# A decode backward kernel: dw2 and the last head's dV stored by GpSimd scatters that skip the first partitions, and plain transfers for these

## Chip, cores and metric

The kernel runs on 1 core of a Trainium2 chip. The metric is the device time of one execution in microseconds: 404.78 us before the change, as the median of 3 runs (404.63 to 404.84).

## The reference

The program is the gradient of a small mixed layer for one token. Attention over a cached K and V of 32 heads x 4096 positions x 128 (bf16) is mixed by a sigmoid gate with a dense layer (640 to 1728 to 640, mish). It returns the output and nine gradients.

```python
def _A_ref(x, k_cache, v_cache, wq, wo):
    q = ...(x @ wq) split into 32 heads
    scores = jnp.einsum("bhqd,bhkd->bhqk", q, k_cache) * (Dh ** -0.5)
    p = _softmax(scores, axis=-1)
    o = jnp.einsum("bhqk,bhkd->bhqd", p, v_cache)
    return o.reshape(B, Sq, H * Dh) @ wo

def _B_ref(x, w1, b1, w2):
    h = x @ w1 + b1
    act = h * jnp.tanh(softplus(h))
    return act @ w2

out = g * a + (1 - g) * b          # g = sigmoid(sum(x * gate_w))
_out, _vjp = jax.vjp(_f, A_x, A_k_cache, A_v_cache, A_wq, A_wo, B_w1, B_b1, B_w2, gate_w)
return (out, *_vjp(grad_out))
```

Most of the bytes are K and V (32 MB each, read) and dK and dV (32 MB each, written). dV of a head is the outer product of its 4096 probabilities and its 128 values of do; dw2 (1728 x 640) is the outer product of the activations and the scaled gradient.

## The kernel before

**Tiling.** A head's K or V is a tile of 128 partitions x 32 positions x 128 (1 MB; partition p holds positions 32p to 32p + 31, so a partition's row is 8,192 B, contiguous in memory). Heads run one after the other in a software pipeline written out by hand: the loop body of head h (lines 743 to 853) transposes K and V of head h + 1 and part of h + 2 on TensorE (`k_pe`, `v_pe`, line 515), evicts them on ScalarE (`ev`, line 524), does the softmax of head h on VectorE, and multiplies out dV (`dv_out`) and dK (`dk_out`) in halves on VectorE (`outer`, line 598).

**Stores.** `out_half` (line 602) picks the output tile, and after the second half stores it through SyncE's queue (line 616). Tiles come from `outs` (4 buffers, o_sb); for the last heads the freed input buffers Kn and Vn are used (dK of heads 28 to 30, dV of heads 29 to 31), so that these need not wait for an earlier store. dK of head 31 goes through o_sb again.

**Queues.** SyncE issues nearly all transfers in program order: loads of K and V four heads ahead, weights, and all large stores. GpSimd issues a few small ones: b1, the rows of h (lines 410, 412), the last 64 rows of dw2 (line 800), db1 (line 802), and at the end three stores of 5 rows each, taken from fin_rows (lines 920 to 922). Each engine takes its instructions in order.

**dw2.** w2 lies in w2_sb as 13 blocks of 640 in each of 128 partitions (a row of 16,640 B, contiguous in memory), and a 14th block of 64 partitions. `m_dw2(fc)` (line 503, on ScalarE) overwrites block fc by the gradient; `dw2_some(2)` at the end of each loop body does two of them, once w2 is no longer read, counting up from `dw2_next[0]`. At head 28 (`h == H - 4`, line 796) all blocks must be done; SyncE then stores blocks 0 to 3, 4 to 7 and 8 to 12 (line 799), GpSimd the 14th and db1. GpSimd's queue is free by then, so line 800 goes out as soon as its data is ready.

**The end.** After the loop: softmax, dV and dK of head 31, then the last dwq (line 377) and dwo (line 386), and the vectors out, dx and dgate, which are gathered in fin_rows.

The order of instructions on each engine is the program's (`manual_schedule`); waits between engines, and between transfers that touch the same memory, are put in by the framework.

Of the kernel before, what the change touches and what calls it, by code (L numbers as in the profile page):

```python
# [8 lines left out]
ALU = mybir.AluOpType  # L9
# [7 lines left out]
def kernel(  # L17
# [24 lines left out]
    nc = tc.nc  # L42
    P = 128
    _, H, Sk, Dh = A_k_cache.shape
# [8 lines left out]
    FR = F // P  # L53
    FM = FR * P
# [4 lines left out]
    W2P = [(0, 4), (4, 8), (8, FR)]  # L59
# [17 lines left out]
    dw2_v = out_8[0:FM, :].rearrange("(p fc) n -> p fc n", p=P)  # L77
# [11 lines left out]
    const = ctx.enter_context(tc.tile_pool(name="const", bufs=1))  # L89
# [59 lines left out]
    w2_sb = const.tile([P, FCN, D], BF16, name="w2_sb")  # L149
    for a, b in W2P:  # L150
# [10 lines left out]
        out=ident_bf[:], in_=ident_bf[:], compare_op=ALU.not_equal, fill=1.0,  # L161
        base=0, pattern=[[-1, P]], channel_multiplier=1,
# [20 lines left out]
    nc.vector.memset(aT_acc[:], 0.0)  # L183
    bT = const.tile([P, RC], F32, name="bT")
    dx_parts = const.tile([P, RC, NG + 3], F32, name="dx_parts")

    p4b, ds4b = [], []
    qz = const.tile([P, G, 2, 2, 16], BF16, name="qz")
# [57 lines left out]
    def g_qpair_cp(g):  # L246
        pair_cp(qz, groups[g].pop("pair"), 4)

    def g_docol(g):
        groups[g]["col"] = col_mm(groups[g]["do_row"])  # L250

    def g_dopair(g):
        groups[g]["pair"] = pair_mm(groups[g].pop("col"))
# [160 lines left out]
    def m_np(fc):  # L414
        return P if fc < FR else FT
# [60 lines left out]
    def m_diag():  # L476
        nc.vector.tensor_copy(dh_bf[:, 0:FR], dh32[:, 0:FR])
        nc.vector.tensor_copy(dh_bf[0:FT, FR:FCN], dh32[0:FT, FR:FCN])
        nc.gpsimd.tensor_tensor(diag3, ident_bf[:].unsqueeze(2).to_broadcast([P, P, FR]),
                                dh_bf[:, 0:FR].unsqueeze(1).to_broadcast([P, P, FR]), ALU.mult)  # L480
        nc.gpsimd.tensor_tensor(mjunk[0:FT, FM:F], ident_bf[0:FT, 0:FT],
                                dh_bf[0:FT, FR:FCN].to_broadcast([FT, FT]), ALU.mult)
# [18 lines left out]
    def m_dw2(fc):  # L501
        n = m_np(fc)
        nc.scalar.activation(w2_sb[0:n, fc, :], db_bc[0:n, :], ACT.Copy, scale=act_f[0:n, fc:fc + 1])
# [14 lines left out]
    def ev():  # L518
        trq.pop(0)()
# [6 lines left out]
    def k_pe(h, c):  # L526
        if h < H:
            tr_pe(h, kts, KT, c)

    def v_pe(h, c):  # L530
        if h < H:
            tr_pe(h, vts, VT, c)
# [32 lines left out]
    def softmax(h):  # L565
        mx = s_ps.tile([P, P + 2], F32, name="mx", tag="mx")
        nc.tensor.transpose(mx[:, 0:P], dgms.pop(h)[:].to_broadcast([P, P]), ident_f[:])  # L567
        negM = small.tile([P, 1], F32, name="negM", tag="negM")
        nc.vector.tensor_reduce(negM[:], mx[:, 0:P], axis=AX.X, op=ALU.max, negate=True)  # L569
        return mx, negM  # L570

    def exps(h, negM):
        es[h] = small.tile([P, J], BF16, name="e_bf", tag="e_bf")
        zds[h] = small.tile([P, 2], F32, name="zd", tag="zd")
        nc.scalar.activation(es[h][:], sd[h][0], ACT.Exp, bias=negM[:], scale=scale, accum_out=zds[h][:, 0:1])  # L575
# [21 lines left out]
    def outer(dst, col4, row, a, b):  # L597
        nc.vector.tensor_tensor(  # L598
            dst[:, a:b, :].rearrange("p j (k t) -> p j k t", t=4),
            row.rearrange("p (k t) -> p k t", t=4).unsqueeze(1).to_broadcast([P, b - a, Dh // 4, 4]),  # L600
            col4[:, a:b, :].unsqueeze(2).to_broadcast([P, b - a, Dh // 4, 4]), ALU.mult)

    o_t = {}

    def out_half(w, h, dst, col4, row, k):
        hh = h % G
        if k == 0:
            if w == "k" and H - KBUFS <= h < H - 1:
                o_t[w, h] = kv_in.tile([P, J, Dh], BF16, name="Kn", tag="Kn")
            elif w == "v" and h > H - VBUFS:  # L610
                o_t[w, h] = kv_in.tile([P, J, Dh], BF16, name="Vn", tag="Vn", bufs=VBUFS)
            else:
                o_t[w, h] = outs.tile([P, J, Dh], BF16, name="o_sb", tag="o_sb")
        outer(o_t[w, h], col4, row[:, hh * Dh:(hh + 1) * Dh], k * JH, (k + 1) * JH)
        if k == 1:
            nc.sync.dma_start(dst[h], o_t.pop((w, h))[:])

    def dv_out(h, k):
        out_half("v", h, dVv, p4s[h], groups[h // G]["do_row"], k)
# [1 line left out]
    def dk_out(h, k):  # L621
        if h >= 0:
            out_half("k", h, dKv, ds4s[h], groups[h // G]["qs_row"], k)
# [12 lines left out]
    def dqo_red(h, x):  # L636
        if h >= 0:
            v = x[:].rearrange("p t r -> p (t r)")[:, 3:3 + 4 * (P - 1)].rearrange("p (s q) -> p s q", q=P - 1)
            nc.vector.tensor_reduce(groups[h // G]["dqo"][:, :, h % G],  # L639
                                    v[:, :, 0:P - 1:32].rearrange("p s (i c) -> p i s c", i=2),  # L640
                                    axis=AX.XY, op=ALU.add)
# [6 lines left out]
    m_cost = dict(h=0.8, b1=0.8, act=0.9, b=0.5, dh=0.9, diag=0.5, bc=0.5, dx=0.9, dw1=0.5, gap=0.0)  # L648
    m_fn = dict(h=m_h, b1=lambda i: (m_b1(), m_abs()), act=m_act, b=m_b, dh=m_dh,
                diag=lambda i: m_diag(), bc=m_bc, dx=m_dx, dw1=m_dw1)  # L650
    dw2_next = [0]

    def mlp_some(budget, pause=True):
        spent = 0.0
# [88 lines left out]
    for h in range(H - 1):  # L743
        g, hh = h // G, h % G
        nx, pv = g + 1 < NG, g > 0
        k_pe(h + 1, 2)
        ev()
        mx, negM = softmax(h)
        if hh == 3 and nx:
            g_qpair_cp(g + 1)  # L750
            g_docol(g + 1)
        dqo_red(h - 1, xs[h])
        k_pe(h + 1, 3)
        ev()
        exps(h, negM)
        dk_out(h - 1, 1)
        v_pe(h + 1, 0)
        if hh == 2 and nx:
            g_q(g + 1)
        v_pe(h + 1, 1)  # L760
        if hh == 3 and nx:
            g_dopair(g + 1)
            g_dopair_cp(g + 1)
        k_rows(h + 1)
        ev()
        ev()
        pjs(h)
        v_pe(h + 1, 2)
        ev()
        zd_mm(h, mx)  # L770
        if hh == 0 and pv:
            f_new(g - 1)
            f_diag(g - 1)
        elif h >= 2:
            mlp_some(0.9, False)
        v_pe(h + 1, 3)
        ev()
        probs(h, mx)
        if hh == 0 and pv:
            f_o4(g - 1)  # L780
            f_o4c(g - 1)
            f_bc(g - 1)
        dv_out(h, 0)
        k_pe(h + 2, 0)
        dq_o(h)
        v_rows(h + 1)
        rw_cp(h + 1)
        if h + 2 < H:
            ev()
        dv_out(h, 1)  # L790
        load_k(h + KBUFS)
        load_v(h + VBUFS)
        k_pe(h + 2, 1)
        if h + 2 < H:
            ev()
        if h == H - 4:
            assert dw2_next[0] == FCN
            for a, b in W2P:
                nc.sync.dma_start(dw2_v[:, a:b, :], w2_sb[:, a:b, :])
            nc.gpsimd.dma_start(out_8[FM:F, :], w2_sb[0:FT, FR, :])  # L800
            assert not any(k == "bc" for k, _ in mq)
            nc.gpsimd.dma_start(db1_row, dh_bc[0:1, :])
        if h == H - 2:
            assert not mq
            nc.sync.dma_start(dw1_v[:, 0:3, :], w1_sb[:, 0:3, :])
            nc.sync.dma_start(dw1_v[:, 3:RC, :], w1_sb[:, 3:RC, :])
        dk_out(h, 0)
        x_tr(h + 1)
        maxes(h + 1)
        if hh == 0:  # L810
            if nx:
                g_new(g + 1)
            if pv:
                l_pe(g - 1, 0, G)
                l_add(g - 1, g - 1, True)
                for t in range(G):
                    f_dwo(g - 1, t)
                f_dwo_st(g - 1)
                for c in range(2):
                    f_dx(g - 1, c)  # L820
                    f_dwq(g - 1, c)
        if hh == 1:
            if pv:
                for c in range(2, RC):
                    f_dx(g - 1, c)
                    f_dwq(g - 1, c)
                f_dwq_st(g - 1)
            if nx:
                w_pe("o", g + 1, 0)
                ev()  # L830
                w_pe("o", g + 1, 1)
                ev()
        if hh == 2:
            if g + 2 < NG:
                load_wo(g + 2)
            if not nx:
                for k in range(NWT):
                    w_pe("q", g, k)
                    ev()
            else:  # L840
                w_pe("o", g + 1, 2)
                ev()
                g_do(g + 1)
                g_qcol(g + 1)
                g_qpair(g + 1)
        if hh == 3:
            if g % 2 == 0 and g + 4 <= NG:
                load_wqp(g // 2 + 1)
            if nx:
                g_qs(g + 1)  # L850
        if h >= 2:
            mlp_some(0.9 if hh < 2 else 1.8)
            dw2_some(2)

    g, h = NG - 1, H - 1
# [97 lines left out]
```

## Time and profile before

| | us |
|---|---|
| median of the runs | 404.78 |
| profiled execution | 404.96 |
| its span | 403.18 |
| PE busy in the span | 305.9 |
| DVE busy | 287.9 |
| ACT busy | 232.4 |
| POOL busy | 11.8 |
| DMA, mean | 408 GB/s over 164.55 MB |
| last issue of dV (head 31) on SyncE | 384.71 |
| last issue of dwo on SyncE | 390.73 |
| first issue of fin_rows on GpSimd | 393.67 |

The span runs from the first instruction of the program to the last one; the profiled execution's own time is 1.78 us longer. An issue is the moment at which an engine's sequencer starts a transfer; its landing is told by a semaphore that each of the 16 DMA engines raises when its share is in, so that a transfer has 16 landing records, and it has landed with the last. The DMA engines work on shares of every transfer: with 128 rows each has 8. Queue q1 is SyncE's, q0 is GpSimd's.

### The profile page before, as it was taken

To read this page: it belongs to the slowest core of one execution; us is meant where nothing else is said; L and a number is where in the kernel's file an instruction comes from. 1 tells how busy PE (TensorE), PEld (TensorE's weight loads), DVE (VectorE), ACT (ScalarE), POOL (GpSimd) and SP (SyncE) were. 2 spreads that over 40 slices of the span, in tenths; PEclk is the share of its full clock that TensorE was granted. 3 is DMA by queue.
4 is the path that set the end of the run, shared out by engine and by line. 5 is a ranking of instruction groups with operands and counts; after the bars stand their busy time and mean duration, and the time that the engine had idled before them with its cause. 6 is when DMAs were issued, how large, how long until landed. Compare 5 with 4: busy or idle time off the path is not lost.

```text
span 403.2 us, 7688 instructions
## 1 busy us (share of the span) xinstructions
PE 305.9 (76%) x2930; PEld 207.0 (51%) x2945; DVE 287.9 (71%) x808; ACT 232.4 (58%) x468; POOL 11.8 (3%) x29
## 2 busy tenths in 40 slices
PE   2979989787897985876887779876886977677640
PEld 1556646464565663544555447544555645464420
DVE  2217738868678875769897956896997985679780
ACT  2466757754676563753668667765767655375220
POOL 3000001000000000000001200000000000000001
PEclk9999999988999998989998997988999899889555
DMA  7999999999999999999999999999999999999894
GB/s 274 428 416 423 417 424 415 417 423 424 422 422 426 423 414 424 424 418 428 422 423 428 424 418 424 427 418 423 422 419 424 425 417 425 426 422 377 360 389 153
DMA packets 28708, 164.55 MB, mean 408 GB/s; under 512 B 2991, under 2 KB 3056, under 8 KB 12288
## 3 DMA queue, kind: packets, MB, share of 16 engines
q1 hardware_dynamic: 28256, 163.97, 98.1%
q8 instruction: 23, 0.38, 0.4%
q0 software_dynamic: 384, 0.10, 0.1%
q14 instruction: 13, 0.11, 0.1%
q10 hardware_dynamic: 32, 0.01, 0.0%
HBM read 82.03 MB, written 82.03 MB: 407 GB/s over the span
## 4 chain that ended last, share of the span: by engine, by line
DMA 42%; PE 25%; DVE 22%; ACT 6%; issue 2%; POOL 0%; POOLq 0%; SPq 0%; DVEq 0%; ACTq 0%
DMA out_dram<-o_sb 40%; PE tr L515 9%; DVE o_sb L598 9%; PE rw L538 3%; PE rw L631 3%; DVE junk L362 3%; DMA wq_p<-in_A_wq_dram 2%; PE x L555 2%; DVE wq_p L372 2%; ACT rw_sb L549 2%; ACT do_row L266 2%; PE tr L324 2%; PE do_ps L263 1%; PE h_ps L405 1%; DVE mjunk L494 1%
## 5 line engine op out<-in xcount | busy, mean ns | idle before, releaser
L524 ACT COPY T<-tr 128x512 f32<-128x512 f32 x256 | 138.0, 595 | 53.0 <-PE tr L515 38.3
L598 DVE TENSOR_TENSOR o_sb<-qs_row,ds 128x2048 bf16<-128x2048 bf16 x58 | 70.8, 1220 | 37.6 <-DMA out_dram<-o_sb 37.5
L515 PE MATMUL tr<-ident_f,Kn 128*128 128x128 f32 x512 | 85.6, 295 | 5.8 <-DVE rw L508 5.8
L515 PE MATMUL tr<-ident_f,Vn 128*128 128x128 f32 x512 | 84.5, 299 | 6.6 <-ACT T L524 6.0
L515 PEld LDWEIGHTS tr<-ident_f,Vn 128*128 128x128 f32 x512 | 63.4, 154 | 27.3 <-PE tr L515 12.1
L515 PEld LDWEIGHTS tr<-ident_f,Kn 128*128 128x128 f32 x512 | 61.1, 149 | 23.2 <-PE rw L631 14.1
L598 DVE TENSOR_TENSOR o_sb<-do_row,p 128x2048 bf16<-128x2048 bf16 x58 | 68.2, 1218 | 0.0
L549 ACT COPY rw_sb<-rw 128x512 f32<-128x512 f32 x33 | 19.4, 587 | 51.2 <-PE rw L538 49.0
L631 PE MATMUL rw<-Kn,ds 128*4 128x512 bf16 x256 | 35.9, 405 | 6.4 <-DVE ds L593 5.7
L631 PE MATMUL rw<-Vn,p 128*4 128x512 bf16 x256 | 35.9, 405 | 0.0
L567 PE MATMUL mx<-ident_f,m_s 128*128 128x128 f32 x32 | 10.1, 316 | 29.7 <-DVE m_s L563 29.6
L555 PE MATMUL x<-ident_f,rw_sb 128*128 128x128 f32 x132 | 22.5, 295 | 4.4 <-ACT rw_sb L549 1.4
L362 DVE SCALAR_TENSOR_TENSOR junk<-wq_p,dq_bc 128x512 bf16<-128x512 bf16 x35 | 23.9, 684 | 0.0
L538 PE MATMUL rw<-T,qz 128*32 128x512 bf16 x256 | 22.3, 426 | 0.0
L575 ACT ACTIVATE e_bf<-x,negM 128x32 bf16<-128x32 f32 x32 | 9.3, 292 | 22.4 <-DVE dqo L639 22.1
L567 PEld LDWEIGHTS mx<-ident_f,m_s 128*128 128x128 f32 x32 | 4.5, 142 | 34.0 <-DVE m_s L563 33.9
L538 PE MATMUL rw<-T,doz 128*32 128x512 bf16 x256 | 21.4, 411 | 0.8 <-ACT T L524 0.8
L380 ACT ACTIVATE wo_g<-da_bc,o 128x640 bf16<-128x640 bf16 x28 | 20.9, 816 | 1.2 <-PE ax_ps L350 1.2
L583 PE MATMUL mx<-zd,ones_f 128*128 128x2 f32 x64 | 11.2, 245 | 13.5 <-DVE pj L579 13.4
L555 PEld LDWEIGHTS x<-ident_f,rw_sb 128*128 128x128 f32 x132 | 14.5, 145 | 13.2 <-ACT rw_sb L549 13.2
L569 DVE TENSOR_REDUCE negM<-mx 128x1 f32<-128x128 f32 x32 | 9.2, 288 | 16.1 <-PE mx L567 16.1
L631 PEld LDWEIGHTS <-ds 128*4 128x4 bf16 x256 | 9.1, 85 | 22.2 <-DVE ds L593 11.4
(174 smaller groups left out, 367.6 us busy)
## 6 DMA issues: line engine op xcount, KB each, us to landing
out_dram<-o_sb SPq DMA_DIRECT2D x58, 1024.0 KB, 16.6
Kn<-in_A_k_cache_dram SPq DMA_DIRECT2D x32, 1024.0 KB, 16.8
Vn<-in_A_v_cache_dram SPq DMA_DIRECT2D x32, 1024.0 KB, 17.3
wq_p<-in_A_wq_dram SPq DMA_DIRECT2D x4, 1280.0 KB, 8.7
wo_g<-in_A_wo_dram SPq DMA_DIRECT2D x8, 640.0 KB, 17.6
out_dram<-wo_g SPq DMA_DIRECT2D x8, 640.0 KB, 18.3
out_dram<-wq_p SPq DMA_DIRECT2D x4, 1280.0 KB, 16.3
out_dram<-Kn SPq DMA_DIRECT2D x3, 1024.0 KB, 11.4
```

Source lines behind the costliest of these rows:

```text
L362: nc.vector.scalar_tensor_tensor(jq[:], in0=wqs[g][:, c, :], scalar=1.0, in1=groups[g]["dq_bc"][:], op0=ALU.mult, op1=ALU.mult, accum_out= ...
L380: nc.scalar.activation(wos[g][:, hh, :], da_bc[:], ACT.Copy, scale=groups[g]["o4"][:, hh:hh + 1])
L515: nc.tensor.transpose(tp[:, t, :], words[:, t * P:(t + 1) * P], ident_f[:])
L524: nc.scalar.copy(T[h][:, (3 - c) * (TB // 2):(4 - c) * (TB // 2), :], tp[:])
L538: nc.tensor.matmul(rw[32 * c:32 * (c + 1), :], lhsT=z[:, par, :, :].rearrange("p m u -> p (m u)"), rhs=Tb[:, c, par, :, :], start=first an ...
L549: nc.scalar.copy(rw_sb[h][:].rearrange("p t r -> p (t r)"), rw[:])
L555: nc.tensor.transpose(xs[h][:, 3 - j, :], t[:, j, :], ident_f[:])
L567: nc.tensor.transpose(mx[:, 0:P], dgms.pop(h)[:].to_broadcast([P, P]), ident_f[:])
L575: nc.scalar.activation(es[h][:], sd[h][0], ACT.Exp, bias=negM[:], scale=scale, accum_out=zds[h][:, 0:1])
L583: nc.tensor.matmul(mx[:, P:P + 2], lhsT=ones_f[:], rhs=zds[h][:], start=True, stop=True)
L598: nc.vector.tensor_tensor(dst[:, a:b, :].rearrange("p j (k t) -> p j k t", t=4), row.rearrange("p (k t) -> p k t", t=4).unsqueeze(1).to_br ...
L631: nc.tensor.matmul(rw[32 * c:32 * c + 4, :], lhsT=c4[:, 4 * jb:4 * jb + 16].rearrange("p (j t) -> p t j", t=4)[:, 0, :], rhs=N[:, jb:jb + ...
```

## The change

The three stores of dw2 by SyncE become one scatter by GpSimd with one row of 16,640 B for each partition, and the store of dV of head 31 becomes another, with one row of 8,192 B for each partition. A scatter takes the target row of each partition from a list in SBUF, `rowids`: p for dw2, 31 x 128 + p for dV. In the first 8 entries (dw2) or 16 entries (dV) the list holds a row beyond the bound (8192), and such a row is not written. A plain transfer, issued by GpSimd right behind the scatter, writes these rows. The list is made on GpSimd at the start by two instructions.

`m_dw2` of block 0 is held back: `dw2_next` starts at 1, and block 0 is scaled at head 28, right before the stores. In GpSimd's order come then: the 64 rows of the 14th block, the scatter and the plain rows of dw2, db1, the scatter and the plain rows of dV, and the three stores of fin_rows.

The target of the dV scatter is all of dV seen as 4096 rows, that of its plain rows the first 16 of head 31; the framework lets the scatter wait for the earlier stores into dV, and the plain rows for the scatter.

```diff
+    SKIP = (8, 16)
+    rowids = const.tile([P, 2], mybir.dt.int32, name="rowids")
+    nc.gpsimd.iota(rowids[:], pattern=[[(H - 1) * P, 2]], base=0, channel_multiplier=1)
+    nc.gpsimd.affine_select(out=rowids[:], in_=rowids[:], compare_op=ALU.is_ge, fill=float(2 * H * P),
+                            base=-SKIP[0], pattern=[[SKIP[0] - SKIP[1], 2]], channel_multiplier=1)
+
+    def scat_st(i, rows, lim, dst, src):
+        ids = rowids[:, i:i + 1].bitcast(mybir.dt.uint32)
+        nc.gpsimd.indirect_dma_start(out=rows, out_offset=bass.IndirectOffsetOnAxis(ap=ids, axis=0), in_=src,
+                                     in_offset=None, bounds_check=lim - 1, oob_is_err=False)
+        nc.gpsimd.dma_start(dst[0:SKIP[i]], src[0:SKIP[i]])
...
         if k == 1:
-            nc.sync.dma_start(dst[h], o_t.pop((w, h))[:])
+            t = o_t.pop((w, h))
+            if (w, h) == ("v", H - 1):
+                scat_st(1, out_3.rearrange("b h (p j) d -> (b h p) (j d)", p=P), H * P,
+                        dst[h].rearrange("p j d -> p (j d)"), t[:].rearrange("p j d -> p (j d)"))
+            else:
+                nc.sync.dma_start(dst[h], t[:])
...
-    dw2_next = [0]
+    dw2_next = [1]
...
         if h == H - 4:
             assert dw2_next[0] == FCN
-            for a, b in W2P:
-                nc.sync.dma_start(dw2_v[:, a:b, :], w2_sb[:, a:b, :])
+            m_dw2(0)
             nc.gpsimd.dma_start(out_8[FM:F, :], w2_sb[0:FT, FR, :])
+            rows = out_8[0:FM, :].rearrange("(p fc) n -> p (fc n)", p=P)
+            scat_st(0, rows, P, rows, w2_sb[:, 0:FR, :].rearrange("p fc n -> p (fc n)"))
             assert not any(k == "bc" for k, _ in mq)
             nc.gpsimd.dma_start(db1_row, dh_bc[0:1, :])
```

## The prediction

> **What bounds the kernel now.** I read the slices of the page first, then its chain of waits, then the last 30 us in windows, and last SyncE's final waits.
>
> ```profile
> span 403.2 us, 7688 instructions
> ...
> DMA  7999999999999999999999999999999999999894
> ...
> DMA 42%; PE 25%; DVE 22%; ACT 6%; issue 2%; POOL 0%; POOLq 0%; SPq 0%; DVEq 0%; ACTq 0%
> ```
>
> The 16 DMA engines are full from the second slice to the last but two. Up to 344 us the chain goes through stores (o_sb buffers that come free late), after that through computation alone. What ends the span is seen in the windows (columns: stretch, length, five engines' busy time, granted clock, DMA share, GB/s):
>
> ```profile
> 369.00:371.00 2.00, 0.27 (x3) 0.08 (x1) 1.87 (x6) 1.33 (x5) 0.00 (x0) 1.00 0.60 252
> ...
> 376.00:388.00 12.00, 7.59 (x68) 5.01 (x67) 8.95 (x26) 3.30 (x9) 0.00 (x0) 0.50 1.01 409
> ...
> 397.00:402.00 5.00, 0.00 (x0) 0.00 (x0) 0.00 (x0) 0.00 (x0) 0.00 (x0) 0.50 0.07 26
> ```
>
> From 397 to 402 us the share is 0.07, one engine of 16 (0.0625), at 26 GB/s. SyncE's last waits say the same: after the small fin_rows stores it still waits 1.0 us and 1.5 us for two large stores.
>
> ```profile
> SPq L948 <- DMA out_dram<-fin_rows: 7.0, 1, 7.0
> ...
> SPq L948 <- DMA out_dram<-wo_g: 1.5, 1, 1.5
> ...
> SPq L948 <- DMA out_dram<-wq_p: 1.0, 1, 1.0
> ```
>
> The landing records of the trace (16 for a transfer, one for each DMA engine) give the reason. For V of head 31 the engines land between 352.6 and 357.1, except one at 362.0. That late engine is 9.8 us behind at 369, where the others run dry (the window at 0.60), and still 5.2 us behind in the last dwo store: the first engines land it at 396.94, the next to last at 397.8, the late one at 402.16. Its packets follow each other without a hole from 354 us to there, so it alone sets the end: 402.16, plus 1.02 to the span's end (403.18), plus 1.78 outside the span makes the profiled 404.96. The median of the runs, 404.78, is 0.18 less.
>
> **The change, part by part.** *What leaves the late engine.* A transfer of 128 rows puts 8 rows on each engine, and a 1 MB one costs each 8 x 0.306 us = 2.45 us by its packet records. A skipped block of 8 rows takes 133 KB of dw2 (8 x 16,640 B, 5.0 us at that rate) and 65.5 KB of dV (2.45 us) off one engine. The plain transfers bring a row of each back: 0.62 + 0.31 us. If the late engine is the one that would carry rows 0 to 7, it gets 6.5 us less work, and ends with the others.
>
> Is it that one? GpSimd's transfers cut rows into consecutive blocks: the 128x13 load of b1 went as 16 packets of 208 B (8 rows of 26 B), the 64x640 store as 16 of 5,120 B (4 rows). The three fin_rows stores have 5 rows each and so use 5 engines, and the late engine carried a 256 B packet of all three (at 397.99, 398.49, 398.99), while the second-latest carried none. So it is one of the five that short transfers use, which I take for the first five blocks. Rows 0 to 7 are then one case in five by count; that the second skip reaches row 16, and a split into half blocks, widen it. I put it above one half, since any small transfer also ends on the first of them. [...]
>
> *What the change adds on ScalarE.* The scaling of block 0 of dw2 moves from about 216 us, where the store-bound chain hides it, to head 28, so that the scatter is not issued at 292 us.
>
> ```profile
> 353.96 1.08 ACT L524 COPY T<-tr 128x512 f32<-128x512 f32 x2
> 355.21 2.99 ACT L380 ACTIVATE wo_g<-da_bc,o 128x640 bf16<-128x640 bf16 x4 [0.17 <-PE ax_ps L350]
> ```
>
> It stands between these two and costs 0.82 us (L503's median), of which 0.17 is idle: the wo_g scaling starts 0.65 us later, and with it T, PE's transposes and everything after, since from here the chain is computation without a gap. So dV31 is ready 0.65 us later, and dK31, dwq, dwo and fin_rows too. Before, that cost would be covered by the late engine's backlog.
>
> *dw2's scatter.* It starts at 356 us instead of 354.5 and takes turns with SyncE's stores on the same engines. The loads of K31 and V31 are in by 354.6 and 357.1 on all engines but the late one; nothing after 344 us waits for a store's buffer; the bytes are the same, and the fast engines have the hole at 369 to 376 for them. I take nothing. GpSimd waits for the scatter before the plain rows, with db1 behind it, for which nobody waits until the end. The index list adds two POOL instructions near 3 us (about 0.3 us each by the affine select's row), ahead of qz's memset, which is needed after 12 us: nothing.
>
> *dV of head 31.* The scatter's rows cover all of out_3, so GpSimd waits for every earlier dV store (dV30 landed at 384.3, earlier without the backlog: no added wait). Then the plain 16 rows wait for the scatter's landing, and behind both in GpSimd's order stand the three fin_rows stores. The trace has no scatter. The rows for its price:
>
> ```profile
> 291.88 0.57 POOL L800 DMA_DIRECT2D out_dram<-w_sb  x1 [68.10 <-ACT w_sb L503]
> ```
>
> ```profile
> out_dram<-o_sb SPq DMA_DIRECT2D x58, 1024.0 KB, 16.6
> ...
> out_dram<-w_sb POOLq DMA_DIRECT2D x1, 80.0 KB, 5.5
> out_dram<-fin_rows POOLq DMA_DIRECT2D x3, 1.2 KB, 4.9
> ```
>
> An issue with 64 rows takes 0.57 us, one with 5 rows 0.50 to 0.53; 128 rows make 0.64, and POOL's longest instruction, 2.99 us (L479), is the other end. From the end of an issue to the first packet GpSimd's transfers took 2.4 us (fin_rows) to 3.8 us (h_sb), SyncE's dK31 about 0.6. I take 0.64 + 3.0: issued at 385.4, first data at 389.0. [...] The scatter lands between 385.4 + 5.5 = 390.9 (the POOL row) and 385.4 + 16.6 = 402.0 (the 1 MB row, with queues full). I take 5.5 + 2.45 for its bytes: 393.3, nearest to the POOL row because SyncE's queue is nearly empty then. The plain rows are issued by 394.0, and fin_rows, due at 393.67 + 0.65 = 394.3, is not held.
>
> *The sum.* On the fast engines: dwo at 396.9, + 0.65 (ScalarE), + 0.3 (a plain row), + 1.7 (idle from 386.9 to 389.0 waiting for the scatter, less the 0.44 hole at 388 that goes) = 399.6; the second-latest engine up to 0.9 more, 400.5, less if its rows are among the 16 skipped. fin_rows: third issue at 395.4, + 3.7 = 399.1 without a late engine. I take 400.0 for the last landing: + 1.02 + 1.78 = 402.8 profiled, **402.6** as a median (-0.18), 0.5% faster. Its own range is 401.7 (first data 0.6 us after the issue, as on SyncE: no idle time, fin_rows ends it at 399.1, 0.9 less) to 403.9 (an issue half way to 2.99 us, 1.2 to 1.3 more).
>
> **The rivals.** *The late engine keeps its share.* If its rows are not skipped it gets the plain rows on top, 0.93 us, and it has no hole to hide them: 404.96 + 0.93 = 405.9 profiled, 405.7 as a median, right at the bound of slower. For it: four of the five low engines; against: the packets above.
>
> *GpSimd's queue becomes the end (slower).* Plain rows and fin_rows wait for the scatter's landing L: the third fin_rows store starts at L + 0.1 + 0.6 + 2 x 0.52 and lands 4.84 later, L + 6.6. That passes 402.16 from L = 395.6, a scatter of 10.2 us, which is just what SyncE's dV31 took before (384.71 to 394.94, on the late engine). At 13 us the end is 405.0 + 2.8 = 407.8, 407.6 as a median. For it: full queues from 390 on; against: POOL's rows of 5 to 6 us.
>
> *Given back.* Relief as forecast, but ScalarE's 0.65, the idle engines and a scatter near 10 us meet: 404.8, no change.
>
> **How the numbers follow.** Forecast 0.55, late engine untouched 0.20, GpSimd's queue 0.17, given back 0.08. Faster by over 0.2% (0.8 us, about what a measurement of this kernel can tell from no change) is the forecast, 0.55; slower is the queue and 0.12 of the untouched case, 0.29; the rest 0.16. The range takes in all but the ends: 401.0 (the forecast's lower end, with ScalarE's 0.65 hidden) to 407.3 (the queue rival but for its worst part).
>
> **What would show it.** Right: no window of 0.06 DMA share at the end, the dwo landing spread near 1 us, SyncE's last wait for fin_rows. The step on ScalarE: wo_g of head 28 starts near 355.9. The scatter: POOL rows at about 385.4, landing near 393. Wrong, first rival: the tail on one engine stays, longer by 0.9. Wrong, second: fin_rows issued after 395. Were the scatter to use few engines or short packets, the DMA packet count would jump, and all of this falls.

## The result and the profile after

The changed kernel takes 407.49 us (median of 5 runs, 407.26 to 407.71), beside 404.63 for the kernel before (5 runs, 404.43 to 404.84): 2.86 us more, a ratio of 1.0071 with a 95% interval of 1.0056 to 1.0085. It is slower, and 0.2 us beyond the upper end of the range. The profiled execution took 407.66, 2.70 more than that of before.

Lines of the changed kernel's page (span; DMA share in 40 slices; GpSimd's queue; shares of the chain of waits by engine):

```profile
span 405.7 us, 7699 instructions
...
DMA  7999999999999999999999999999999999998984
...
q0 software_dynamic: 736, 3.28, 2.3%
...
DMA 44%; PE 23%; DVE 22%; ACT 6%; issue 2%; POOL 0%; POOLq 0%; SPq 0%; DVEq 0%; ACTq 0%
```

The end is longer, not shorter. The windows of the changed kernel (columns as before: stretch, length, five engines' busy time, granted clock, DMA share, GB/s):

```profile
369.00:371.00 2.00, 1.21 (x13) 0.52 (x12) 1.96 (x7) 0.33 (x3) 1.23 (x2) 1.00 1.04 328
376.00:388.00 12.00, 7.90 (x64) 5.42 (x64) 8.66 (x27) 2.89 (x8) 1.41 (x1) 0.50 0.90 363
...
397.00:402.00 5.00, 0.00 (x0) 0.00 (x0) 0.00 (x0) 0.00 (x0) 2.06 (x4) 0.50 0.48 141
402.00:405.70 3.70, 0.00 (x0) 0.00 (x0) 0.00 (x0) 0.00 (x0) 0.00 (x0) 0.50 0.02 7
```

Before, the stretch from 397 to 402 had one engine in 16 at work and nothing on GpSimd. Now GpSimd issues four transfers in it. Its timeline and its waits show why so late:

```profile
356.64 1.06 POOL L195 DMA_INDIRECT out_dram<-w_sb,rowids  x1 [64.66 <-ACT w_sb L515]
369.22 0.61 POOL L197 DMA_DIRECT2D out_dram<-w_sb  x1 [11.52 <-DMA out_dram<-w_sb,rowids]
...
386.43 1.41 POOL L195 DMA_INDIRECT out_dram<-Vn,rowids  x1 [15.98 <-DVE dx_parts L370]
398.10 0.54 POOL L197 DMA_DIRECT2D out_dram<-Vn  x1 [10.27 <-DMA out_dram<-Vn,rowids]
398.62 0.52 POOL L938 DMA_DIRECT2D out_dram<-fin_rows  x1
```

The plain rows of dV wait 10.27 us for the scatter, and fin_rows stands behind them: 398.62 instead of 393.67. The chain ends in the same way (start, length, engine, what):

```profile
383.36 2.35 DVE Vn L610 x2
385.80 0.63 issue
386.43 11.39 DMA out_dram<-Vn,rowids
398.10 0.54 POOL out_dram L197
398.64 0.51 POOL out_dram L938
```

and SyncE's last wait is for fin_rows:

```profile
SPq L966 <- DMA out_dram<-fin_rows: 11.7, 1, 11.7
```

Who is late in the scatter? The landing records of the trace (first landing, and in us behind it the second, the eighth, the next to last and the last of 16):

```
                              first    2nd   8th  15th  16th
before  V of head 31 (load)   352.6    0.1   1.6   4.5   9.4
        dK of head 29         374.5    0.0   0.1   1.4   7.2
        dwo                   396.9    0.0   0.1   0.9   5.2
after   V of head 31 (load)   352.9    0.1   1.6   3.8  12.0
        dK of head 29         375.6    0.0   0.0   0.8   7.2
        scatter of dV         390.3    0.0   1.0   1.3   7.5
        dwo                   397.9    0.0   0.9   1.1   5.5
        plain rows of dV      400.3    0.2   0.4   0.9   3.3
        third fin_rows        401.1    0.0   0.3   0.7   3.1
```

The late engine is still there, as late as before (7.2 us at dK of head 29, 5.5 at dwo). Fifteen engines have their rows of the dV scatter by 391.6, the late one at 397.82. The plain rows and fin_rows, which need only a little of the engines, wait for that one landing. Four engines land the dV scatter about 1.0 us ahead of the others (390.3 to 390.4, the fifth at 391.3), and two the dw2 scatter (361.2 and 361.9, the third at 363.7). That fits 16 skipped rows that are half the rows of four engines, and 8 that are half those of two.

The 2.70 us of the profiled executions: the last landing moved from 402.16 (dwo) to 404.19 (fin_rows), 2.03; from there to the end of the span it took 1.49 instead of 1.02, 0.47; outside the span 1.98 instead of 1.78, 0.20.

### The profile page after: what moved, and what is told of

The parts are those of the page before. It is cut to its first block, busy times and chain, and to the rows that moved or that the text cites. A ratio compares the mean times of both kernels' runs of the same rounds, so it can differ in the third digit from the quotient of the medians.

```text
span 405.7 us, 7699 instructions
## 1 busy us (share of the span) xinstructions
PE 311.1 (77%) x2930; PEld 212.1 (52%) x2945; DVE 287.8 (71%) x808; ACT 233.1 (57%) x468; POOL 15.9 (4%) x35
## 4 chain that ended last, share of the span: by engine, by line
DMA 44%; PE 23%; DVE 22%; ACT 6%; issue 2%; POOL 0%; POOLq 0%; SPq 0%; DVEq 0%; ACTq 0%
DMA out_dram<-o_sb 39%; PE tr L527 9%; DVE o_sb L610 9%; PE rw L550 3%; DMA out_dram<-Vn,rowids 3%; DVE junk L374 3%; PE rw L648 3%; DMA wq_p<-in_A_wq_dram 2%; PE x L567 2%; DVE wq_p L384 2%; PE tr L336 2%; ACT wo_g L392 1%; ACT rw_sb L561 1%; ACT do_row L278 1%; PE do_ps L275 1%
## 5 line engine op out<-in xcount | busy, mean ns | idle before, releaser
L527 PE MATMUL tr<-ident_f,Vn 128*128 128x128 f32 x512 | 88.3, 309 | 8.7 <-ACT T L536 8.1
L527 PE MATMUL tr<-ident_f,Kn 128*128 128x128 f32 x512 | 86.6, 298 | 5.7 <-DMA Kn<-in_A_k_cache_dram 5.7
L527 PEld LDWEIGHTS tr<-ident_f,Vn 128*128 128x128 f32 x512 | 67.0, 161 | 29.4 <-PE tr L527 12.0
L527 PEld LDWEIGHTS tr<-ident_f,Kn 128*128 128x128 f32 x512 | 62.0, 151 | 22.7 <-PE rw L648 13.7
```

The source lines that it names most:

```text
L527: nc.tensor.transpose(tp[:, t, :], words[:, t * P:(t + 1) * P], ident_f[:])
```

## The experiments

All start from the changed kernel unless said otherwise. Times are medians; the kernel before was run beside them each time (404.73 to 404.79). The first four ask which part costs what, and which rows the late engine carries.

**e1: the dw2 part alone.**

```diff
-            if (w, h) == ("v", H - 1):
+            if False:          # dV of head 31 by SyncE
```

> dV of head 31 goes back to a plain store on SyncE; dw2 stays a scatter with its skip and the held-back block. Theory A (the slow queueing engine, the late one, still carries 8 rows of each scatter, and the landing of the dV scatter there holds GpSimd's plain rows and the three fin_rows stores): nothing but db1 is behind GpSimd any more, fin_rows is issued near 394.5, and the end is the late engine's, 402.16 plus at most one row of 0.62 us: 404.6 to 405.3. Theory B (a scatter is dear in itself, by its issue and its late first data): half of the loss or more stays, 406 or above. Theory C (the 0.65 to 0.7 us on ScalarE shift the end): 405.3 and the dwo landing moved by 0.7.

Measured: 406.07 (405.82 to 406.61), ratio 1.0030 (1.0017 to 1.0043). The last landing is dwo on the late engine at 403.04, 0.88 later than before; fin_rows is issued at 394.6 and landed by 400.9. So the late engine alone makes the end here. It is above what A expected: the last landing is 0.26 later than the one row of 0.62 us put in, and from it to the end of the span it takes 1.20 us instead of 1.02.

**e2: the dV part alone.** dw2 goes by the three SyncE stores, block 0 is scaled early as before.

```diff
-            m_dw2(0)
+            for a, b in W2P:
+                nc.sync.dma_start(dw2_v[:, a:b, :], w2_sb[:, a:b, :])
...
-            scat_st(0, rows, P, rows, w2_sb[:, 0:FR, :]...)
```

> dw2 goes back to three stores on SyncE with nothing held back; dV of head 31 stays a scatter with 16 skipped rows and plain rows behind it. Theory A: issued at about 385.5, the scatter lands on the late engine some 11 us later, at 396.5 to 397, and the last fin_rows store lands 6.4 us after that, near 403.2: 405.8 to 406.5. Theory B: the same sign, but then the first landings would be late as well, 6 us or more after the issue. Theory C: no loss, 404.6, since nothing is added on ScalarE.

Measured: 406.20 (406.08 to 406.50), ratio 1.0034 (1.0021 to 1.0046). The scatter, issued at 385.4, landed between 391.5 and 396.3, the plain rows were issued at 396.5, and the last fin_rows landed at 402.72: GpSimd's queue is the end, at the time that A gave. Its first landing came 6.1 us after the issue, though, which had been set as the sign of B. The packets give a plainer reason: the scatter's data starts at 389.83, when the packets of dK of head 31, which SyncE issued at 386.31, have ended on most engines. In the changed kernel that store comes behind the scatter, and the first landing takes 3.9 us. The two halves cost 1.31 and 1.44 us beside the kernel before; the whole change cost 2.86.

**e3: both scatters with all 128 rows, no plain transfers.**

```diff
-    SKIP = (8, 16)
+    SKIP = (0, 0)
...
-        nc.gpsimd.dma_start(dst[0:SKIP[i]], src[0:SKIP[i]])
```

> Both scatters write all 128 rows, and no plain rows follow. Theory A: the late engine has the same bytes as before the change, and fin_rows waits for no landing and is issued near 394.7; the late engine ends near 402.5: 404.6 to 405.3, although it has lost every relief. Theory B: both scatters are still there, so 406.5 or more.

Measured: 405.76 (405.56 to 406.06), ratio 1.0022 (1.0012 to 1.0032). fin_rows goes out at 394.5 as forecast, and the last landing (dwo, late engine) is 402.30, only 0.14 later than before. The time lies 0.46 us above A's range and 0.74 below B's. At the end the scatters delay nothing, as the late engine hides what they cost the others (the first engine lands dwo at 398.70 instead of 396.94). What is left of the loss lies behind the last landing, 1.28 us to the end of the span and 2.09 outside it (before: 1.02 and 1.78).

**e4: whose rows are they?** Four stores as scatters of half the rows: dw2 without the rows whose number has bit 6 set, dK of head 29 without bit 4, dV of head 30 without bit 3, dK of head 31 without bit 2. The rows left out stay unwritten; dV of head 31 goes by SyncE.

> Half of the rows of four stores are left unwritten: dw2 leaves out the rows with bit 6 of the partition set (64 to 127), dK of head 29 those with bit 4, dV of head 30 those with bit 3, dK of head 31 those with bit 2. [...] If the split were in blocks of 8 consecutive rows, bit 2 would leave every engine 4 rows. [...]

It took 404.44 us (one execution). The late engine's packets follow each other nearly without a hole, so they can be followed back from its last landing. Of each store it carried:

```
store            rows left out     its packets on the late engine
dw2              bit 6 = 1         8   (361.3 to 368.0 us)
dK of head 29    bit 4 = 1         0
dV of head 30    bit 3 = 1         8   (385.0 to 387.2)
dK of head 31    bit 2 = 1         8   (397.2 to 399.5)
```

All or nothing each time, so its 8 rows have bit 6 = 0, bit 4 = 1, bit 3 = 0 and bit 2 = 0: rows 16 to 19 and 48 to 51. The change skips rows 0 to 7 and 0 to 15 and stops one row short of them. The late engine is called engine 4 from here on, and the one with rows 20 to 23 and 52 to 55 (f4) engine 5, both by their first row divided by four: no trace numbers the engines, and which rows the other 14 have was not shown.

The next four move the right rows.

**f1: the change with the rows of engine 4.** Both scatters skip rows 16 to 19 and 48 to 51, and two plain transfers of 4 rows each bring them back. (The list for such rows is made by four small instructions on VectorE at the start, here and in the runs below that skip rows.)

```diff
-        nc.gpsimd.dma_start(dst[0:SKIP[i]], src[0:SKIP[i]])
+        for a in (16, 48):
+            nc.gpsimd.dma_start(dst[a:a + 4], src[a:a + 4])
```

> The change as it is, but both scatters skip rows 16 to 19 and 48 to 51 (by the run before, those of the late engine), and two plain transfers of 4 rows each bring them. Theory A (the late engine is number 4 and ended the run because the skipped rows were not its own): it loses 5.0 + 2.45 us of work, the one-engine tail goes, the dV scatter lands near 391.7 instead of 397.8, fin_rows is issued near 394.7, and the last landing is near 399.7: 403.0 to 404.0, faster than before. Theory B (scatters are dear in themselves): 406 or more, whatever rows are skipped.

Measured: 406.79 (406.68 to 407.60), ratio 1.0053 (1.0032 to 1.0074). A miss: the right rows alone do not save the change. The dV scatter now lands from 393.6 to 396.36 (one engine, at 391.15, apart), with other engines late, and the plain rows again go out only at 396.64, the last fin_rows landing at 403.13.

**f2: the same for dw2 alone.** 

> Only dw2 is a scatter, skipping the 8 rows of engine 4; dV of head 31 stays a plain store on SyncE. Theory A: the late engine loses 5.0 of the 5.2 us it is behind at the end, the last landing is at 398.5 to 399.2, and with 1.2 us to the span's end and 1.8 outside it the time is 401.5 to 402.3. Theory B: as the run with rows 0 to 7 skipped, 406.

Measured: 405.17 (404.94 to 405.79), ratio 1.0010 (1.0001 to 1.0020). Another miss, and the most telling. Engine 4 is relieved: it was 9.4 us behind at V of head 31, and at dK of head 28, a large store issued behind the scatter at 360.0, no engine is more than 3.6 behind. But four engines then fall 7.4 to 8.2 us behind at the plain rows (issued at 368.26 and 368.86), and dwo lands from 399.2 to 402.3. The packet records of that time (start in us, ns, queue, bytes; some of many):

```
f2      370.34  2788  q0 16640      after   370.41  2284  q0 16640
        370.80  4052  q0 16640              370.55  2196  q0 16640
        373.13  4953  q0 16640              370.66  2287  q0 16640
        373.16  4985  q0 16640              372.63   946  q0 16640
        375.69   611  q1  8192
        376.30   611  q1  8192
```

In a scatter a packet of 16,640 B takes 0.62 to 0.66 us (95% of them in e3's, the longest 0.80). In the plain transfers it takes up to 2.4 us in the changed kernel and up to 5.0 in f2. One engine's SyncE packets of 8,192 B next to it, six in a row from 374.47 to 378.13, take 0.61 instead of 0.31.

The author's account of this is where the bytes are read. In a scatter engine 4 reads the 8 partitions that are its own (e4: 8 packets or none). In a plain transfer of 4 rows four engines would read one engine's partitions: 4 x 0.62 = 2.5 us if they share what one engine gets from there (rows 0 to 7 of the changed kernel are, by its two early landings, four each of two engines). f2 fits four readers too: its eight plain packets never run more than four at a time, and the last four each begin where one of the first four ends (370.34 + 2.79 = 373.13). The 5.0 us come while the 0.61 us packets run, which are taken here for engine 4's own share of dK of head 29, from the same partitions. If these get half of the rate and the four readers the other half, a row takes 2 x 4 x 0.62 = 5.0 us and one of these packets 2 x 0.31 = 0.62, near the 0.61. By this account rows handed to other engines are still read at the late engine's partitions, and hold up those that read them. It is an estimate from the packets' times; that the partitions are what is shared was not shown, as no run reads the same bytes from others.

**f4: the same with the next engine's rows,** 20 to 23 and 52 to 55, as a control. 

> As the run with dw2 alone and engine 4's rows, but the rows of engine 5 (20 to 23 and 52 to 55) are skipped: same instructions, same bytes. Theory A: no relief where it counts, the one-engine tail stays: 404.8 to 406.1. If skipping any 8 rows helps, or if the relief is not the reason, it equals the engine 4 run.

Measured: 405.53 (405.26 to 406.13), ratio 1.0017 (1.0007 to 1.0026), in the range of A. Now one engine is 4.9 us ahead of the rest at the scatter, close to the 8 x 0.62 = 5.0 us of a whole engine's rows, and the late engine stays 10.2 us behind, 5.4 at the end. The rows do decide who is relieved.

**f3: f2 with everything earlier.** Block 0 is scaled at the end of the loop body of head 27, so the scatter is issued at 341.99 and the plain rows at 354.86, while K and V of head 31 are still being loaded.

```diff
-            m_dw2(0)           # head 28
...
+            if h == H - 5:     # end of head 27
+                m_dw2(0)
```

> As the run before, but block 0 of dw2 is scaled at the end of head 27's loop body instead of between the evictions of head 28. If ScalarE's 0.7 us at head 28 shift the end once the late engine is out of the way (theory C), this is 0.5 to 0.8 us faster than the run before: 400.8 to 401.7. If the scatter's earlier start slows the loads of K and V of head 31, it is not faster.

Measured: 403.19 (402.58 to 404.69), ratio 0.9955 (0.9940 to 0.9970): faster than the kernel before. It is 1.5 us above the upper end of what was expected; in the profiled execution, its slowest (404.69), the earlier bytes delay the loads of head 31, and dK of head 29 is issued at 373.8 instead of 370.8.

Four more ask whether the plain rows, the time of issue or the queue is behind this.

**g1: f2 without the plain rows.** 

> dw2's scatter alone at head 28 (dV of head 31 by SyncE), skipping rows 16-19 and 48-51, and no plain transfer: these 8 rows of dw2 stay unwritten, so the time is that of a store of 120 rows. A, the port theory (the plain rows are read from the 8 partitions of the late engine, and all engines that carry them share the rate at which these 8 can be read): without the plain rows nobody is blocked, the late engine has 5 us less to read, no engine is 7 us behind at 370-379 us, the last landing is at 398.5-399.5 and the time 401.3-402.5. B, the late engine's lag is not made of its own bytes, or the four engines of the f2 kernel fell behind for another reason: the late landings stay near 402 and the time near f2's 405.2.

Measured: 402.45 (402.24 to 402.82), ratio 0.9945 (0.9928 to 0.9962), in the range of A. At dK of head 29 (375.3) the engines lie within 0.6 us but for one at 1.6. With the plain rows the same kernel took 405.17: it is they that hold the others up.

**g2: engine 4's rows first.** They go by four transfers of 2 rows at the end of head 27; a small rewrite on ScalarE holds the scatter back to head 28.

```diff
+            if h == H - 5:
+                m_dw2(0)
...
+                for a in (16, 18, 48, 50):
+                    nc.gpsimd.dma_start(rows[a:a + 2], src[a:a + 2])
...
-            m_dw2(0)
+            nc.scalar.activation(w2_sb[:, 0, 0:2], db_bc[:, 0:2], ACT.Copy, scale=act_f[:, 0:1])
```

> dw2 alone; rows 16-19 and 48-51 go first, by four GpSimd transfers of 2 rows at the end of head 27 (about 342 us), and the scatter of the other 120 rows follows at head 28 as in the change. A, the port theory: the 8 rows are read while the loads of K31 and V31 keep the engines writing, so the blocking costs little and the late engine has 5 us less from 360 us on: 402.0-403.7, the better the fewer engines are still 4 us behind at 368 us. B, moving the rows gains nothing and the f3 kernel's gain came from issuing the whole of dw2 earlier: 404.5-405.5, as with the plain rows behind the scatter.

Measured: 401.66 (401.42 to 401.98), ratio 0.9922 (0.9906 to 0.9939): 3.1 us faster than before, 0.3 below A's range, and the best of all. GpSimd's timeline and two windows of this kernel:

```profile
341.99 2.08 POOL L881 DMA_DIRECT2D out_dram<-w_sb  x4 [118.02 <-ACT w_sb L519]
...
355.52 1.61 POOL L200 DMA_INDIRECT out_dram<-w_sb,rowids  x1 [10.90 <-ACT w_sb L819]
```

```profile
369.00:371.00 2.00, 0.28 (x3) 0.10 (x1) 1.85 (x6) 1.35 (x5) 0.00 (x0) 1.00 0.77 325
397.00:402.00 5.00, 0.00 (x0) 0.00 (x0) 0.00 (x0) 0.00 (x0) 0.00 (x0) 0.50 0.01 2
```

The tail on one engine is gone: 0.01 where before had 0.07. The landings say it too: V of head 31 still has an engine 10.1 us late, at dK of head 29 the last is 2.8 us behind, at dwo 0.9 (397.0 to 397.9), and fin_rows ends the run at 398.4. Of the 8 packets of engine 4's rows five take 0.62 to 0.63 us, the other three 1.59 to 2.51. That at most two engines read these partitions at once here is the author's estimate, from the two rows of a transfer.

**g3: the change with fin_rows on ScalarE's queue.**

```diff
-    nc.gpsimd.dma_start(out0_rows, fin_rows[0:RC, :])
+    nc.scalar.dma_start(out0_rows, fin_rows[0:RC, :])     # and the other two
```

> The change as it is, but the three fin_rows stores are issued from ScalarE's queue, so that they don't stand behind the plain rows of dV. A, two causes in the change (a late engine that keeps all its bytes, dwo's last landing 403.4, and GpSimd's queue, fin_rows' last landing 404.2): dwo or the plain dV rows (403.6) become the end, the time is 406.4-407.2, 0.4-1.0 less than the change. B, GpSimd's queue alone makes the loss: about 404.8, as before.

Measured: 406.99 (406.69 to 407.62), ratio 1.0058 (1.0041 to 1.0074), as A has it. fin_rows is out of the queue behind the scatter, and dwo (403.6) and the plain dV rows (403.3), both on the late engine, are the end at once. GpSimd's queue is only 0.5 us worse than the late engine itself.

**g4: f3 with the rows of engine 5.** 

> Control for the f3 kernel: the same early issue of dw2's scatter at the end of head 27, but with the rows of the neighbouring engine (20-23 and 52-55) in the plain transfers. A, f3's gain of 1.6 us is relief of the late engine: here its tail stays, dwo lands last near 402 and the time is 404.5-406. B, the gain is that of storing dw2 earlier, whatever the rows: 402.8-403.7, as f3.

Measured: 405.40 (405.14 to 406.48), ratio 1.0024 (1.0014 to 1.0035). This is in the range of A: the earlier time alone gains nothing; with engine 4's rows it gained 1.6 us.

Two last ones look at what e1 and e3 had left over, from the kernel before.

**h1: dw2 as one scatter of 128 rows,** nothing else changed. 

> The kernel before, but the three stores of dw2 are one GpSimd scatter of all 128 rows: no row skipped, no plain rows, nothing moved on ScalarE, dV by SyncE. A, an indirect store has a price of its own behind the last landing (e3: 1.28 us to the end of the span and 2.07 outside it, where before had 1.02 and 1.78): 405.1-405.6. B, e3's extra time came from its dV scatter or from the scaling moved to head 28: 404.5-404.9.

Measured: 408.07 (407.21 to 408.71), ratio 1.0079 (1.0065 to 1.0093). Neither theory: the run did not isolate what it was meant to. With block 0 scaled early, the scatter's data is ready at 293 us and GpSimd's queue is free, so 2 MB are stored there, amid the loads:

```profile
293.34 1.06 POOL L195 DMA_INDIRECT out_dram<-w_sb,rowids  x1 [0.42 <-DMA out_dram<-o_sb]
```

The last load of V lands at 369.4 instead of 362.0, and dwo is issued at 396.3 instead of 390.7. It shows what the moved scaling is for in the change, and what it would cost to leave it out.

**h2: only the scaling of block 0 at head 28.** 

> The kernel before, but block 0 of dw2 is scaled at head 28, as in the change; all stores as before. A, the late engine's backlog hides ScalarE's 0.65 us: 404.5-405.0. B, the delay is not hidden: 405.3-405.6.

Measured: 404.85 (404.51 to 405.20), ratio 1.0000 (0.9991 to 1.0009): nothing. The late engine is still the end (dwo 402.10), as its window says:

```profile
397.00:402.00 5.00, 0.00 (x0) 0.00 (x0) 0.00 (x0) 0.00 (x0) 0.00 (x0) 0.50 0.06 25
```

What e1 and e3 had left is told in part by comparing all traces: profiled time less span was 1.98 to 2.19 us in the six kernels with a scatter into dK or dV (the changed one, e2, e3, e4, f1, g3), and 1.78 to 1.82 in the ten without (before among them). Why is open, and so is the rest, 0.26 us from e3's last landing to the end of its span.

## Why the prediction was wrong

**"What bounds the kernel now" was right.** One engine's backlog set the end. When it is relieved without harm (g2), the tail goes and the kernel gains 3.1 us; the forecast had 2.2 from the same mechanism, as it charged the fast engines 0.65, 0.3 and 1.7 us of delays, the last two of which belong to the dV part that g2 leaves alone.

**"Is it that one?" was the step that failed.** It took GpSimd's plain transfers (b1: 16 packets of 208 B, 8 rows each) as the rule for a scatter, and the five-row stores as proof that the late engine has one of the first five blocks. That any small transfer ends on the first of the five too was an assumption: db1, a single row of 3,456 B, went as 16 packets of 216 B. A scatter gave the late engine two groups of four partitions, 32 apart (e4: rows 16 to 19 and 48 to 51, 8 packets or none); the two and four early engines of the changed kernel fit the same cut. By them the first 16 rows are half the rows of four other engines. So 6.5 us of relief became none, and the plain rows came on top: at the end the late engine still lands dwo 5.5 us behind the first, and the scatter of dV 7.5 behind.

**Relief would not have followed from the right rows either.** The prediction counted a plain row as 0.62 us (dw2) and 0.31 (dV) on each engine. They took up to 2.4 and 1.1 us in the changed kernel, 5.0 in f2; the account above, that several engines read one engine's partitions, is an estimate. f2 (405.17) against g1 (402.45), which leaves out these rows alone, shows that price; g2 (401.66) shows that it need not be paid. There the rows went earlier, while loads ran, and two to a transfer instead of four; the two were not tried apart.

**ScalarE, 0.65 us.** wo_g of head 28 starts at 356.22, where 355.9 was forecast. Two lines of the changed kernel's timeline:

```profile
354.54 1.08 ACT L536 COPY T<-tr 128x512 f32<-128x512 f32 x2
355.49 0.85 ACT L515 ACTIVATE w_sb<-db_bc,act_f 128x640 bf16<-128x640 bf16 x1
```

wo_g starts 1.01 us later than before, not 0.65. T starts 0.58 later, ahead of the moved instruction; from T to wo_g it is 1.68 instead of 1.25, so the instruction itself costs 0.43. The late engine hides it, as was said (h2: nothing).

**dw2's scatter, "I take nothing": right** for the scatter (e3: last landing 0.14 later), wrong for its plain rows (e1: 0.88).

**dV's scatter.** Two terms were off and nearly cancelled. It is issued at 386.43, not 385.4: its data is ready 1.0 us later than before, and GpSimd starts 0.63 us behind that (the `issue` step in the chain above). The issue takes 1.41 us, not 0.64. But its first packet starts at 388.41, 0.57 us behind the end of the issue, where 3.0 was taken from plain GpSimd transfers; that is the 0.6 of the range's lower end. So the fast engines run dry from 387.0 to 388.4, 1.4 us, where 1.7 was taken. They land dwo at 397.9 (four of them, with half of their dV rows skipped) or at 398.8 to 399.0 (eleven), where the sum had 399.6. On 15 engines the scatter is in at 391.6, earlier than the 393.3 forecast. On the late one it is in at 397.82: its eight packets run from 392.66 to 397.00, from 393.6 on in turn with SyncE's, one in 0.61 us. The forecast for it held for an engine without a backlog, and there the backlog was to be gone.

**The rival that came true** is "GpSimd's queue becomes the end": fin_rows lands 6.37 us after the scatter, where L + 6.6 was worked out, and its 407.6 is the time. The error in the weights is that this case and "the late engine keeps its share" were priced as two. They are one: if the late engine keeps its rows, it lands the scatter late too, as it had landed SyncE's dV of head 31 at 394.94, close to the 395.6 from which the queue decides. Its 0.20 belonged to the queue's side. Its sum had L = 398.4 in it, a scatter of 13 us; L was 397.82, 0.6 less, and 0.7 us more lay behind the last landing; that 407.6 and 407.49 come so close is in part luck.

## What to carry to other kernels

When one DMA engine sets the end, find out which rows it carries before moving rows: leave some rows of a scatter out, by bits of the partition number, and count its packets. Rows moved to other engines are still read from the same partitions; sent four or eight to a transfer behind the large store they were slow here (up to 2.4 us for 16,640 B in the changed kernel and 5.0 in f2, where a scatter's packet takes 0.62), and four engines fell 7.4 to 8.2 us behind in f2. Sent ahead in transfers of two rows, while loads ran (g2, 401.66 us), they did little harm; behind the large store (f2, 405.17, beside 402.45 without them in g1) they took back the gain. And do not put small last stores in a queue behind a wait for a large one: here it took 10.27 us, until 398.10, with 15 of the 16 engines in by 391.6 and the slowest at 397.82.

## What the runs showed of the hardware

- One engine of 16 fell 9 us or more behind the first by the loads of head 31 in every trace (9.4 in the kernel before, 12.0 in the changed one, 9.4 in f2, 10.1 in g2). Where it can be told which (e4 by its packets; f2, f3, g1 and g2 by its relief), it is the one with rows 16 to 19 and 48 to 51. In the kernel before, the lag of the last engine grows over the whole run: 0.5 us at the first load, 2.5 at 79 us, 5.0 at 190, 9.0 at 338. Why, and why this engine, stays open.
- Packets of 16,640 B took 0.62 to 0.66 us in a scatter (95% of e3's), up to 2.4 in the plain transfer of 8 rows of the changed kernel, and up to 5.0 in the two of 4 rows of f2, where up to four ran at a time and one engine's packets of 8,192 B beside them took 0.61 instead of 0.31. That four engines then share the rate of one engine's partitions is the author's estimate from these times.
- A scatter with 128 rows occupies GpSimd for 0.97 to 1.84 us (its list has 128 entries, written or skipped), a plain transfer of 2 to 16 rows for 0.5 to 0.6.
- Kernels with a scatter into dK or dV take 1.98 to 2.19 us outside the span, all others 1.78 to 1.82. Why is open.
